# Small chunk inside the first wide chunk's steps, seven products in more second layers, and a scale applied at PSUM

## The chip, the cores and the metric

The kernel runs on one core of one Trainium2 chip. The metric is the device time of one execution in microseconds (us); lower is better. The engines are TensorE (PE; its weight loads are PEld), VectorE (DVE), ScalarE (ACT), GpSimd (POOL) and SyncE (SP), which issues the DMAs.

## What is computed

Three stages follow each other on 4 x 576 = 2304 tokens of 512 numbers: windowed attention (8 heads of 64), an MLP that mixes tokens and then a channel MLP 512 -> 1536 -> 512, and a second channel MLP 512 -> 2048 -> 512 on normalized input scaled by g.

```python
def _moe_ref(x, w_tok1, w_tok2, w_ch1, w_ch2):
    xt = x.transpose(0, 2, 1)
    h = np.maximum(xt @ w_tok1, 0.0) @ w_tok2
    u = x + h.transpose(0, 2, 1)
    h2 = np.maximum(u @ w_ch1, 0.0) @ w_ch2
    return (u + h2).astype(np.float32)

def _moe2_ref(x, g_ln, w_ch1, w_ch2):
    mu = np.mean(x, axis=-1, keepdims=True)
    var = np.mean((x - mu) ** 2, axis=-1, keepdims=True)
    xn = (x - mu) / np.sqrt(var + 1e-06) * g_ln
    ch = np.maximum(xn @ w_ch1, 0.0) @ w_ch2
    return (x + ch).astype(np.float32)
```

The weights arrive as float64 and are converted on the chip. Every matmul operand is split into a high and a low part (float32r), and a product is three matmuls: high x high, high x low, low x high.

## The kernel before

**Tiles, chunks and steps.** The 2304 tokens are 18 tiles of 128. They stay in SBUF as `u` (one buffer for all 18). After attention and the token mixing, which end near 200 us, the two channel MLPs run in steps. A step takes two blocks of 128 hidden features for one chunk of tiles. The chunks are tiles 0 to 7 (wide), 16 and 17 (small), 8 to 15 (wide), in this order, for the first MLP (6 steps each) and then the second (8 steps each): 42 steps.

**First layer of a step.** For a wide chunk, `seven_products` (L1122) computes 256 features x 1024 tokens in seven products of half-size blocks, in place of eight: 7 x 6 = 42 matmuls of 512 columns. Its inputs are 14 operand pairs (seven for each half of the contraction), made by `prep_wide` (L902) from transposes of `u` (`turned`, L873; for the second MLP ScalarE normalizes into `st` first, L883), and weight sums made by `w1_of` (L975). For the small chunk, `two_blocks` (L1223) does 24 matmuls of 256 columns.

**Second layer of a step.** `second` (L1236) does six matmuls of 512 columns for each tile (48 for a wide chunk, 12 for the small one) and adds the result to `u` on VectorE (L1256). In the last chunk of the second MLP, for all steps but the last, `second_fast` (L1261) computes it in seven products as well: for two groups of tiles, 84 matmuls of 256 columns (L1288) and twelve additions (L1307). It needs sums of hidden blocks (`parts_of`, L1172), and sums of second-layer weights, which `keep_sums` (L1058) makes on GpSimd in the first wide chunk and stores to DRAM; `sums_of` (L1100) loads them. Some of its products begin from a copy in a second PSUM bank (`fork`, L1293), which is opened by one extra matmul after transposes have used that bank (L1300). The second layer of a step runs among the first-layer products of the next step; the numbers in `ns` say how many units of it follow each pair of products.

**Weights.** `load_f64` (L411) loads a block in two halves and converts it with one ScalarE and four VectorE operations (L449 to L464). `stage_w` (L538) converts blocks ahead and keeps them in DRAM at `STAGE_RATES` a step; `load_w` (L526) loads six blocks ahead, from DRAM where a block is kept. First-layer blocks of the second MLP are multiplied by g after conversion (`convert_w`, L506, L516). `w_split` makes high and low parts: ScalarE makes the high (L385), GpSimd (L403, two instructions of half width) or VectorE (L401) the low part.

**Order of work.** Each operation is handed to a planner with its cost and the engines that may do it. It computes due times backwards from TensorE's work (`ranks`), then simulates all engines in time and fixes the engine of each operation and the order on every queue. Each queue runs in that order: an instruction that waits holds those behind it. SP's DMA issues are one such queue; `shift_wt1` (L583) issues six copies of first token-mixing weights, shifted by 64 rows, from GpSimd.

Of the kernel before, what the change touches and what calls it, by code (L numbers as in the profile page):

```python
# [51 lines left out]
FAST2 = ((1, 2),)  # L52
# [56 lines left out]
class Part(Buf):  # L109


    def __init__(self, whole, get):
        self.plan, self.pool, self.spec = whole.plan, whole.pool, whole.spec
        self.ops, self.track, self.after, self.behind, self.first = [], {}, [], None, set()
        self.whole, self.get = whole, get
# [6 lines left out]
class Plan:  # L122
# [32 lines left out]
    def op(self, cost, emit, reads=(), writes=(), behind=()):  # L155
        k = len(self.ops)
        deps, behind = set(behind), set()
        for group, write in ((reads, False), (writes, True)):
            for x in group:
# [11 lines left out]
                assert not getattr(b, "closed", False), f"{b.spec[2]} is used after its place was given away"  # L171
                assert write or any(w for key2, (w, _) in b.track.items() if key is None or key2 in (None, key)), \
                    f"{b.spec[2]} is read before it is written"
                b.ops.append(k)
                for key2, (ws, rs) in b.track.items():
# [162 lines left out]
def block_kernel(tc, qT, kT, v, wt1, wt2, wa1, wa2, wb1, wb2, g, bias, out):  # L338
# [13 lines left out]
    for name in ("const", "big", "wa", "raw", "cvt", "small", "hid"):  # L352
        open_pool(name)
# [12 lines left out]
    g_sb = buf("const", [P, DM // P, 1], F32, "g_sb")  # L366
# [6 lines left out]
    u_all = buf("big", [P, NTILE, DM], F32, "u")  # L373
    u = [Part(u_all, lambda t, i=i: t[:, i]) for i in range(NTILE)]
# [131 lines left out]
    def convert_w(x, dst=None, get=None):  # L506

        m, f = x
        if m != "b1":
            return load_f64(src[m], f, DM, dst, get)  # L510
        y, gy = load_f64(src[m], f, DM)
        if dst is None:
            dst, get = y, gy

        def scale(e):
            ENGINE[e].tensor_tensor(get().rearrange("p (k f) -> p k f", k=4), gy().rearrange("p (k f) -> p k f", k=4),  # L516
                                    g_sb.t.to_broadcast([P, 4, P]), ALU.mult)

        pl.op({"DVE": dve(DM), "POOL": pool_tt(DM)}, scale, [y, g_sb], [dst])
        return dst, get  # L520
# [187 lines left out]
    def normalize(i):  # L708
# [13 lines left out]
        minus(u[i], lambda: u[i].t.rearrange("p (h d) -> p h d", h=H), pv,  # L722
# [3 lines left out]
    def x_tile(i):  # L726
# [3 lines left out]
        split(xh, lambda: xh.t, xl, lambda: xl.t, u[i], lambda: u[i].t, DM, ("ACT",),  # L730
# [32 lines left out]
    def tok2(i):  # L763
# [18 lines left out]
        op({"DVE": dve(DM)}, lambda: nc.vector.tensor_tensor(u[i].t, o.t, u[i].t, ALU.add), [o], [u[i]])  # L782
# [6 lines left out]
    def attention():  # L789
# [37 lines left out]
        for i in range(-1, NTILE + 1):  # L827
# [15 lines left out]
            for c in range(2):  # L843
# [10 lines left out]
                if n == 1:  # L854
                    load_bias(2, 4)
                    load(g_sb, lambda: g_sb.t.rearrange("p k o -> p (k o)"), P * DM // P * 4, g)
# [16 lines left out]
    def turned(layer, places):  # L873
# [4 lines left out]
        get = [lambda i=i, k=k: u[i].t[:, k * P:(k + 1) * P] for i, k in places]  # L878
# [17 lines left out]
    def split_x(x, b, psum):  # L896

        hi, lo = x
        copy(hi, lambda: hi.t, b, lambda: b.t, CW, ("ACT",), psum)
        minus(lo, lambda: lo.t, b, lambda: b.t, hi, lambda: hi.t.bitcast(F32), CW, ("DVE",) if psum else ("DVE", "POOL"))  # L900

    def prep_wide(layer, tiles):  # L902
# [12 lines left out]

        def temp():
            return buf("mlp", [P, CW], F32, "st", ST_BUFS)

        def pieces(kk):
            b11, b12 = quadrant(0, 0, kk), quadrant(0, 1, kk)  # L920
            c12, t1 = temp(), temp()
            copy(c12, lambda: c12.t, b12, lambda: b12.t, CW, ("ACT",), True)
            split_x(part(0, kk), b11, True)
            minus(t1, lambda: t1.t, c12, lambda: c12.t, b11, lambda: b11.t, CW, ("DVE",))
            split_x(part(3, kk), t1, False)
# [3 lines left out]
            minus(t2, lambda: t2.t, b22, lambda: b22.t, t1, lambda: t1.t, CW, ("DVE",))  # L929
# [564 lines left out]
```

## Time and profile before

| | us |
|---|---|
| three runs | 833.47, 833.73, 835.28 |
| median | 833.73 |
| profiled execution, its own time | 835.53 |
| its span, first to last instruction | 833.8 |
| TensorE busy | 821.5 |
| VectorE busy | 659.1 |
| GpSimd busy | 466.9 |
| ScalarE busy | 428.5 |

The durations come from the profiled execution. In rows of instructions the second number is the duration; instructions of one engine overlap a little, so the distance between starts is shorter. An arrow `<-` names inputs, or, in rows of waits, what ended the wait. "x84" counts instructions.

### The profile page before, as it was taken

What the parts mean: (1) busy time and instruction counts of PE and PEld (TensorE: products, weight loads), DVE (VectorE), ACT (ScalarE), POOL (GpSimd) and SP (SyncE); (2) the same over time, 40 slices, a digit from 0 to 9 for tenths busy, and PEclk for the clock granted to TensorE, in tenths of its full rate; (3) what the DMA queues carried; (4) which work ended last, traced back from release to release, by engine and by line L of the source; (5) the groups of instructions that cost most, each with busy time, mean ns of one, the idle gap of its engine ahead of it and who ended that gap; (6) DMA issues with size and microseconds to landing.
All of it is one profiled execution on the core that took longest, in us unless ns stands there. A gap on an engine that the chain in (4) does not pass through costs nothing.

```text
span 833.8 us, 14352 instructions
## 1 busy us (share of the span) xinstructions
PE 821.5 (99%) x4732; PEld 693.4 (83%) x4732; DVE 659.1 (79%) x1379; ACT 428.5 (51%) x1015; POOL 466.9 (56%) x723
## 2 busy tenths in 40 slices
PE   8999999999999999999999999999999999999998
PEld 6777788888888898888888888888889889999996
DVE  5888777978787989987889868989666767777785
ACT  5888677643344535334368333447456634444430
POOL 2785466756354567544248666857533656666640
PEclk9999999999999999999999999999999999999999
DMA  9679645454678899987861544888977663443302
GB/s 328 191 184 306 232 140 191 143 186 144 216 226 297 293 317 322 339 293 240 280 238 54 188 154 139 290 309 300 354 263 237 226 226 130 137 141 116 102 26 101
DMA packets 80474, 179.21 MB, mean 215 GB/s; under 512 B 9104, under 2 KB 10768, under 8 KB 80400
## 3 DMA queue, kind: packets, MB, share of 16 engines
q1 hardware_dynamic: 79920, 176.98, 62.9%
q0 software_dynamic: 480, 1.31, 0.7%
q8 instruction: 37, 0.61, 0.3%
q14 instruction: 37, 0.30, 0.1%
HBM read 138.15 MB, written 38.80 MB: 212 GB/s over the span
## 4 chain that ended last, share of the span: by engine, by line
PE 92%; DVE 4%; ACT 3%; DMA 1%; issue 1%; POOL 0%; DVEq 0%; ACTq 0%; POOLq 0%
PE tok L1253 10%; PE tok L1251 10%; PE b L1138 10%; PE tok L1252 10%; PE b L1139 10%; PE b L1140 10%; PE tok L1288 5%; PE p L1288 4%; PE ps_s L636 3%; PE ps_v L648 3%; PE p L891 2%; PE b L482 2%; PE b L481 2%; PE b L480 2%; PE ps_t L693 1%; ACT pr L686 1%
## 5 line engine op out<-in xcount | busy, mean ns | idle before, releaser
L1256 DVE TENSOR_TENSOR u<-tok,u 128x512 f32<-128x512 f32 x196 | 134.4, 687 | 52.5 <-PE tok L1253 51.1
L1251 PE MATMUL tok<-w2h,hh 128*128 128x512 f32 x392 | 154.0, 393 | 0.0
L1253 PE MATMUL tok<-w2h,hl 128*128 128x512 f32 x392 | 152.9, 390 | 0.2 <-DVE hl L971 0.2
L1252 PE MATMUL tok<-w2l,hh 128*128 128x512 f32 x392 | 152.8, 390 | 0.0
L1138 PE MATMUL b<-xh,w1h 128*128 128x512 f32 x384 | 150.4, 392 | 0.3 <-DVE b L401 0.3
L1139 PE MATMUL b<-xl,w1h 128*128 128x512 f32 x384 | 149.8, 390 | 0.0
L1140 PE MATMUL b<-xh,w1l 128*128 128x512 f32 x384 | 149.6, 389 | 0.0
L403 POOL TENSOR_TENSOR w1l<-w,w1h 128x256 fp32r<-128x256 f32 (+1 forms) x112 | 78.9, 726 | 111.4 <-ACT w1h L385 103.4
L969 ACT ACTIVATE hh<-b 128x512 fp32r<-128x512 f32 (+1 forms) x112 | 58.7, 542 | 136.8 <-PE b L1140 95.5
L1253 PEld LDWEIGHTS tok<-w2h,hl 128*128 128x128 f32 x392 | 73.6, 188 | 16.4 <-DVE hl L971 0.8
L1251 PEld LDWEIGHTS tok<-w2h,hh 128*128 128x128 f32 x392 | 73.7, 188 | 15.1 <-DVE u L1256 0.8
L971 DVE SCALAR_TENSOR_TENSOR hl<-b,hh 128x512 fp32r<-128x512 f32 (+1 forms) x112 | 67.2, 617 | 23.9 <-ACT hh L969 23.2
L1252 PEld LDWEIGHTS tok<-w2l,hh 128*128 128x128 f32 x392 | 73.7, 188 | 14.3
L1140 PEld LDWEIGHTS b<-xh,w1l 128*128 128x128 f32 x384 | 72.1, 188 | 15.4
L1138 PEld LDWEIGHTS b<-xh,w1h 128*128 128x128 f32 x384 | 72.2, 188 | 14.6 <-DVE b L401 0.7
L1139 PEld LDWEIGHTS b<-xl,w1h 128*128 128x128 f32 x384 | 72.2, 188 | 13.5
L449 ACT ACTIVATE e<-rh 128x512 bf16<-128x512 bf16 (+2 forms) x62 | 39.7, 641 | 69.4 <-DMA rh<-wb 22.2
L403 POOL TENSOR_TENSOR w1l<-st,w1h 128x256 fp32r<-128x256 f32 x58 | 44.9, 795 | 47.9 <-ACT w1h L385 42.0
L686 ACT ACTIVATE pr<-t,mn 128x128 f32<-128x128 f32 x144 | 55.8, 391 | 14.1 <-DVE mn L677 14.0
L704 POOL TENSOR_SCALAR_AFFINE_SELECT pf<-pf 128x512 f32<-128x512 f32 x64 | 42.1, 659 | 34.6 <-ACT pf L385 28.3
L401 DVE TENSOR_TENSOR b<-b,p 128x512 f32<-128x512 f32 x56 | 38.9, 695 | 20.1 <-PE b L1140 19.5
L403 POOL TENSOR_TENSOR xl<-st,xh 128x256 fp32r<-128x256 f32 x48 | 39.0, 834 | 21.0 <-ACT xh L385 16.6
(193 smaller groups left out, 1919.9 us busy)
## 6 DMA issues: line engine op xcount, KB each, us to landing
w<-d SPq DMA_DIRECT2D x86, 256.0 KB, 4.2
rw<-wb SPq DMA_DIRECT2D x32, 512.0 KB, 5.4
rh<-wb SPq DMA_DIRECT2D x32, 512.0 KB, 5.2
rw<-wa SPq DMA_DIRECT2D x24, 512.0 KB, 4.3
rh<-wa SPq DMA_DIRECT2D x24, 512.0 KB, 4.3
d<-y SPq DMA_DIRECT2D x30, 256.0 KB, 5.3
keys<-kT SPq DMA_DIRECT2D x18, 256.0 KB, 4.6
q<-qT SPq DMA_DIRECT2D x18, 256.0 KB, 4.9
```

The source lines that it names most:

```text
L403: ENGINE[e].tensor_tensor(get()[:, c], ga()[:, c], gb()[:, c], alu)
L686: op({"ACT": 580}, lambda m=m: nc.scalar.activation(out=pr.t[:, m], in_=t.t[:, m], func=AF.Exp, bias=mn.t[:, m:m + 1], scale=-1.0, accum_o ...
L969: op({"ACT": act(n, True)}, lambda: nc.scalar.activation(out=hh.t[:, c], in_=go(), func=AF.Relu), [o], [(hh, key)])
L971: mark[0] = op({"DVE": dve(n)}, lambda: nc.vector.scalar_tensor_tensor(out=hl.t[:, c], in0=go(), scalar=0.0, in1=hh.t[:, c].bitcast(F32), ...
L1138: nc.tensor.matmul(g.t, wh.t[:, w], xh.t, start=start and k == 0, stop=False, skip_group_check=True)
L1139: nc.tensor.matmul(g.t, wh.t[:, w], xl.t, start=False, stop=False, skip_group_check=True)
L1140: nc.tensor.matmul(g.t, wl.t[:, w], xh.t, start=False, stop=stop and k == 1, skip_group_check=True)
L1251: nc.tensor.matmul(o.t, hh.t[:, c:c + P], wh.t, start=j == 0, stop=False)
L1252: nc.tensor.matmul(o.t, hh.t[:, c:c + P], wl.t, start=False, stop=False)
L1253: nc.tensor.matmul(o.t, hl.t[:, c:c + P], wh.t, start=False, stop=j == 1)
L1256: op({"DVE": dve(DM)}, lambda o=o, i=i: nc.vector.tensor_tensor(u[i].t, o.t, u[i].t, ALU.add), [o], [u[i]])
L1288: nc.tensor.matmul(o.t[:, p], x()[:, c], y(), start=start and p == 0 and k == 0, stop=stop and p == 1 and k == 2, skip_group_check=True)
```

## The change

The wide chunks become tiles 2 to 9 and 10 to 17; tiles 0 and 1 are the small chunk. There are 28 steps: the first wide chunk and the second, for each MLP. In each step of the first wide chunk the first layer of the small chunk (`small_block`) is done with the same split weight blocks, after the third pair of products and after the last product, and its two tiles are two further units of the second layer. For this the fourth first-layer block is split whole. The small chunk's inputs have places of their own.

In the first wide chunk of the second MLP the second layer of steps 1 to 6 is done in seven products too. The weight sums are then used where `keep_sums` makes them, in a pool `rows`. Tiles 10 to 17 rest in that pool: after the first step of that chunk, their statistics made, they are stored to DRAM (`put_away`), their places hold sums, and in its last step they are loaded back (`bring_back`). `u` is nine buffers of two tiles.

The scale g is no longer multiplied into the weights; it is applied where the transposed input is copied from PSUM, as a column operand of ScalarE copies and VectorE remainders. The inputs of a wide chunk are all prepared in the last step of the chunk before. Staging in the first chunk goes from 0 to 3 blocks a step. The shifted weight copies are issued by SP instead of GpSimd.

```diff
-W1_BUFS, W2_BUFS, ST_BUFS, H_BUFS = 4, 4, 6, 6
+W1_BUFS, W2_BUFS, ST_BUFS, H_BUFS = 4, 4, 6, 7
+SCRATCH = 2048
+RESTING = range(10, 18)
+SMALL, WIDE = range(2), {0: range(2, 10), 2: range(10, 18)}
-STAGE_RATES = {(0, 2): 2, (1, 0): 2}
+STAGE_RATES = {(0, 0): 3, (0, 2): 2, (1, 0): 2}
-FAST2 = ((1, 2),)
+FAST2 = {(1, 2): range(7), (1, 0): range(1, 7)}
...
-        for c, tiles in enumerate((range(8), (16, 17), range(8, 16))):
+        for c, tiles in WIDE.items():
...
-                nc.gpsimd.dma_start(out=b.t[D:], in_=a.t[:D])
-                nc.gpsimd.dma_start(out=b.t[:D, 1:], in_=a.t[D:, :4])
-                nc.gpsimd.dma_start(out=b.t[:D, 0], in_=a.t[D:, 4])
-
-            op({"POOL": 3900}, emit, [(a, k) for k in range(5)], [b])
+                x, y = a.t.bitcast(F32), b.t.bitcast(F32)
+                nc.sync.dma_start(out=y[D:], in_=x[:D])
+                nc.sync.dma_start(out=y[:D, 1:], in_=x[D:, :4])
+                nc.sync.dma_start(out=y[:D, 0], in_=x[D:, 4])
+
+            op({"DMA": 1820}, emit, [(a, k) for k in range(5)], [b])
...
+    def copy_x(dst, get, b, gb, f):
+
+        if f is None:
+            return copy(dst, get, b, gb, CW, ("ACT",), True)
+        op({"ACT": act(CW, True, 1)}, lambda: nc.scalar.activation(
+            out=get(), in_=gb(), func=AF.Copy, scale=g_sb.t[:, f]), [b, g_sb], [dst])
+
+    def less(dst, get, b, gb, a, ga, f):
+
+        if f is None:
+            return minus(dst, get, b, gb, a, ga, CW, ("DVE",))
+        op({"DVE": dve(CW)}, lambda: nc.vector.scalar_tensor_tensor(
+            out=get(), in0=gb(), scalar=g_sb.t[:, f], in1=ga(), op0=ALU.mult, op1=ALU.subtract), [b, g_sb, a], [dst])
...
-            w3 = w_split("w1", W1_BUFS, f2, right(f2), HW)
+            w3 = w_split("w1", W1_BUFS, f2) if whole else w_split("w1", W1_BUFS, f2, right(f2), HW)
...
+    def in_rows():
+
+        x, y = (buf("rows", [P, 2, DM], F32R, "r", len(RESTING) // 2) for _ in range(2))
+        return [[(z, k), lambda z=z, k=k: z.t[:, k]] for z in (y, x) for k in range(2)]
...
+    def put_away(tiles):
+        for i in tiles:
+            d = resting[i] = buf("dram", [P, DM], F32, f"r{i}")
+            op({"DMA": 728}, lambda x=u[i], d=d: nc.sync.dma_start(out=d.t, in_=x.t), [u[i]], [d])
+
+    def bring_back(tiles):
+        for i in tiles:
+            if i % 2 == 0:
+                pair_of_rows(i // 2)
+            op({"DMA": 728}, lambda x=u[i], d=resting[i]: nc.sync.dma_start(out=x.t, in_=d.t), [resting[i]], [u[i]])
...
         product(6, bd, False, end)
         out(0, 1, bd)
         yield
+        if small:
+            hid["small"] = hidden()
+            small_block(0, ws[0][0], small, hid["small"])
+            yield
         product(5, bb, False, end)
         out(1, 0, bb)
+        if small:
+            yield
+            small_block(1, ws[5][0], small, hid["small"])
         yield
...
+        ns = (6, 8, 0, 0) if before and fast2(before[0]) else (2, 3, 3, 0)
+        if c == 0:
+            ns = (6, 8, 0, 2) if before and fast2(before[0]) else (2, 3, 3, 2) if fast2(s) else (2, 3, 3, 0, 1, 1)
...
+        if before and n == 0 and steps[s - 1][0] == 0:
+            done = steps[s - 1][2]
+            for tiles in (done, SMALL) if steps[s - 1][1] == 0 else (done,):
+                todo.extend((tile_stats, i) for i in tiles)
+                todo.append((chunk_stats, tiles))
+            if layer == 1:
+                while todo:
+                    do_next()
+                put_away(RESTING)
+        if (layer, c) == (1, 0) and n == NF2 // 2 - 1:
+            bring_back(RESTING)
...
+        if end:
             while todo:
                 do_next()
-            if c == 0:
-                xs = prep_small(layer, steps[s + 1][2])
-            else:
-                xs, pieces = prep_wide(1, steps[s + 1][2])
-                for _ in pieces:
-                    pass
+            xs, pieces = prep_wide(*steps[s + 1][::2])
+            for _ in pieces:
+                pass
+            if steps[s + 1][1] == 0:
+                small = prep_small(1, SMALL)
```

## Rows read from the trace of the kernel before

**Rows 1.** The page, part 1: busy time, share of the span, instructions:
```profile
PE 821.5 (99%) x4732; PEld 693.4 (83%) x4732; DVE 659.1 (79%) x1379; ACT 428.5 (51%) x1015; POOL 466.9 (56%) x723
```

**Rows 2.** Waits of TensorE, 200 to 834 us: total, times, longest:
```profile
PE tok L1288 <- DVE u L1256: 0.4, 1, 0.4
PE b L1138 <- DVE b L401: 0.3, 1, 0.3
PE tok L1253 <- DVE hl L971: 0.2, 1, 0.2
```

**Rows 3.** Timeline of TensorE: start us, us; 156 matmuls apart:
```profile
229.70 0.39 PE L1251 MATMUL tok<-w2h,hh 128*128 128x512 f32 x1
...
265.06 1.03 PE L891 MATMUL p<-ident,u 128*128 128x128 f32 x8
```

**Rows 4.** The chain that ended last, one same place in two successive steps:
```profile
708.33 1.43 PE tok L1288 x12
...
727.91 1.43 PE tok L1288 x12
```

**Rows 5.** Timeline of TensorE, small chunk: one same place in two steps:
```profile
625.05 0.28 PE L480 MATMUL b<-fewh,w1h 128*128 128x256 f32 x1
...
630.69 0.28 PE L480 MATMUL b<-fewh,w1h 128*128 128x256 f32 x1
```

**Rows 6.** Stretches: us; busy PE, PEld, DVE, ACT, POOL (instructions); clock, DMA share, GB/s:
```profile
70.00:80.00 10.00, 8.62 (x80) 6.72 (x76) 8.19 (x40) 8.68 (x31) 5.73 (x14) 1.00 0.92 312
...
322.00:342.00 20.00, 19.68 (x86) 15.77 (x85) 18.92 (x38) 7.74 (x14) 15.72 (x25) 1.00 0.97 351
...
443.00:463.40 20.40, 20.40 (x98) 16.59 (x97) 19.57 (x35) 15.02 (x33) 16.06 (x26) 1.00 0.28 94
...
524.60:545.00 20.40, 20.24 (x90) 16.44 (x89) 19.15 (x32) 7.92 (x15) 17.59 (x28) 1.00 0.83 288
...
708.33:727.91 19.58, 19.58 (x128) 17.81 (x128) 14.70 (x23) 9.16 (x17) 12.97 (x20) 1.00 0.40 135
```

**Rows 7.** Groups of VectorE by line and shape: busy, mean ns, idle before:
```profile
L1256 DVE TENSOR_TENSOR u<-tok,u 128x512 f32<-128x512 f32 x196 | 134.4, 687 | 52.5 <-PE tok L1253 51.1
...
L456 DVE TENSOR_SCALAR m<-rw 128x512 uint32<-128x512 uint32 x56 | 32.8, 586 | 0.9 <-DMA rw<-wb 0.7
...
L464 DVE SCALAR_TENSOR_TENSOR y<-m,s 128x512 f32<-128x512 uint32 x36 | 29.5, 819 | 1.2 <-POOL w L516 0.9
...
L454 DVE SCALAR_TENSOR_TENSOR s<-e,s 128x256 int32<-128x256 int32 x56 | 29.3, 524 | 0.2
...
L452 DVE TENSOR_SCALAR s<-e 128x256 int32<-128x256 int32 x56 | 21.6, 385 | 2.7 <-ACT e L449 2.5
```

**Rows 8.** Groups of GpSimd by line and shape:
```profile
L403 POOL TENSOR_TENSOR w2l<-w,w2h 128x256 fp32r<-128x256 f32 x42 | 33.8, 826 | 15.7 <-ACT w2h L385 15.5
...
L403 POOL TENSOR_TENSOR fewh<-fewh,fewl 128x256 fp32r<-128x256 f32 x28 | 22.7, 836 | 0.0
...
L403 POOL TENSOR_TENSOR fewh<-w,fewh 128x128 f32<-128x128 f32 x28 | 14.1, 526 | 0.0
```

**Rows 9.** Groups of ScalarE by line and shape:
```profile
L883 ACT ACTIVATE st<-u,nmr,rstd 128x128 f32<-128x128 f32 x72 | 29.5, 488 | 0.0
...
L385 ACT ACTIVATE xh<-p 128x512 fp32r<-128x512 f32 x24 | 14.2, 597 | 10.7 <-PE p L891 5.8 <-DVE st L401 3.4 <-PE b L1140 1.5
```

**Rows 10.** DMA issues (KB, us to landing); SP queue's waits after 210 us:
```profile
d<-y SPq DMA_DIRECT2D x30, 256.0 KB, 5.3
...
SPq L1051 <- PE tok L1288: 35.0, 13, 11.7
```

**Rows 11.** Timeline of GpSimd, first issue of the shifted copies:
```profile
53.30 0.76 POOL L587 DMA_DIRECT2D wt1h<-wt1h  x1
```

**Rows 12.** Timeline of GpSimd in the first wide chunk, second MLP:
```profile
512.88 1.89 POOL L403 TENSOR_TENSOR w2l<-w,w2h 128x256 fp32r<-128x256 f32 x2
...
518.16 1.43 POOL L403 TENSOR_TENSOR w2l<-w,w2h 128x256 fp32r<-128x256 f32 x2
```

More of the change, by code (lines that the diff above doesn't have):

```diff
@@ L113, in __init__ @@
         self.plan, self.pool, self.spec = whole.plan, whole.pool, whole.spec
-        self.ops, self.track, self.after, self.behind, self.first = [], {}, [], None, set()
+        self.ops, self.track, self.after, self.behind, self.first = [], {}, whole.after, whole.behind, set()
         self.whole, self.get = whole, get
@@ L170, in op @@
                     behind.add(b.behind.ops[0])
-                assert not getattr(b, "closed", False), f"{b.spec[2]} is used after its place was given away"
+                assert not getattr(getattr(b, "whole", b), "closed", False), f"{b.spec[2]} is used after its place was given away"
                 assert write or any(w for key2, (w, _) in b.track.items() if key is None or key2 in (None, key)), \
@@ L350, in open_pool @@
         pl.pools[name] = tc.alloc_tile_pool(name=name, **{"bufs": 1, **kw})
-    for name in ("const", "big", "wa", "raw", "cvt", "small", "hid"):
+    for name in ("const", "big", "rows", "wa", "raw", "cvt", "small", "hid"):
         open_pool(name)
@@ L977, in w1_of @@
         f1, f2 = take_w(), take_w()
-        if len(steps[s][2]) == 2:
-            out = [w_split("w1", W1_BUFS, x) for x in (f1, f2)]
-            keep_taken(2)
-            return out
+        whole = steps[s][1] == 0
         if ahead == "few":
@@ L1053, in w2_of @@
             out.append(x)
-        if c == 0 and (layer, 2) in FAST2 and n < (NF1, NF2)[layer] // 2 - 1:
-            keep_sums(layer, n, wtiles[used[0] - 2:used[0]], last)
-        return sums_of(layer, n, out) if fast2(s) else out
-    def keep_sums(layer, n, w, last):
+        if c == 0:
+            if n not in FAST2.get((layer, 2), ()):
+                return out
+            places = in_rows() if fast2(s) else in_few()
+            keep_sums(layer, n, wtiles[used[0] - 2:used[0]], last, *places)
+            return with_sums(out, *quarters(*places)) if fast2(s) else out
@@ L1096, in keep_sums @@
+        for k, (l, gl), (h, gh) in ((0, lo0, hi0), (1, lo1, hi1)):
+            if k:
+                sub(0, half(x0, 1), half(x1, 1))
+                sub(1, half(x1, 0), part(1))
+            else:
+                sub(0, half(x0, 1), half(x0, 0))
+                sub(1, half(x1, 1), part(0))
+            split(h, gh, l, gl, f, lambda: f.t, DM, ("ACT",), ("POOL",))
+            for p, z, gz in (("h", h, gh), ("l", l, gl)):
                 op({"DMA": 728}, lambda k=k, p=p, gz=gz: nc.sync.dma_start(
-                    out=d[p].t[:, k * DM:(k + 1) * DM], in_=gz().bitcast(F32)), z, [(d[p], k)], last)
+                    out=d[p].t[:, k * DM:(k + 1) * DM], in_=gz().bitcast(F32)), [z], [(d[p], k)], last)
@@ L1454, in block_kernel @@
         pl.emit()
-    for n in ("mlq", "mlr", "mlp", "even", "psc", "pst", "psm", "hid", "small", "cvt", "raw", "wa", "big", "const", "dram"):
+    for n in ("mlq", "mlr", "mlp", "even", "psc", "pst", "psm", "hid", "small", "cvt", "raw", "wa", "rows", "big", "const", "dram"):
         pl.pools[n].release()
```

213 lines of the change are left out of this document (107 added, 106 removed).

## The prediction

> **What bounds the kernel now.** I read the page first: TensorE is busy 99% of the span, the next engine, VectorE, 79% [rows 1]. So time can be won only by fewer or shorter matmuls, and lost only by making TensorE wait. The waits say where it waits today: after 200 us only three times, 0.9 us together [rows 2]. Then the pace. From 229.70 to 265.06 stand 156 back-to-back matmuls of 512 columns, 226.7 ns each [rows 3]. A step of a wide chunk has 42 of them in its first layer and 48 in its second: 90 x 0.2267 = 20.40 us. Where the second layer is done in seven products (tiles 8 to 15, second MLP), 84 matmuls of 256 columns stand for the 48, and the chain repeats every 19.58 us [rows 4]. A step of the small chunk repeats after 5.64 us [rows 5]. These periods contain what is lost at each change of width, so I use them and not durations of single matmuls, which overlap.
>
> **The change part by part.**
> *Seven products in six more steps.* Six steps go from 20.40 to 19.58 us on TensorE: 6 x 0.82 = -4.9. The second-layer banks must be opened again in the first wide chunk: two more matmuls of 512 columns (line 1300) at the pace of rows 3, +0.45. The Trainium skill (TensorE: Matmul & The Clock Gate, Back-to-back issue gap) puts an isolated gap at N/2.4 + 2.5 ns; as an estimate from that page a step would save 48 x 215.8 - 84 x 109.2 ns = 1.19 us, the six 7.1, and the sum below would end at 828.6. The trace shows slower paces for both widths, 226.7 ns for 512 columns, and decides.
>
> *Small chunk inside the wide steps.* Its matmuls stay, 5.64 us a step, 14 times: 0. What goes is its own weight work: in each of its steps two loads of first-layer blocks, four of second-layer parts, two splits; 84 loads of 256 KB in all. The hand-over from small to wide chunk at 322 to 342 us, with VectorE busy 18.9 of 20, left TensorE idle 0.32 us [rows 6]; that place disappears: -0.3 (bounds 0 and -0.9, the three waits of rows 2).
>
> *Load of VectorE and GpSimd in the new steps.* This is the main unknown. A step with seven products now holds 14.70 us of VectorE and 12.97 of GpSimd [rows 6]. In the first wide chunk of the second MLP there come on top, for VectorE: two float64 conversions (385 + 524 + 586 + 819 ns = 2.31 each) 4.6, two more additions of 687 ns 1.4, two ReLU remainders of half width, at most as long, 1.4 [rows 7]: 22.1. For GpSimd: the weight sums, eight pieces of 0.526 and four of 0.836, 7.6; the low parts of two second-layer blocks, four of 0.826, 3.3; half a block more of the first layer, under one such piece, 0.8 [rows 8]: 24.7. Together 46.8 of 2 x 25.2 us (19.58 + 5.64), 93% at most; the planner can move the low parts between the two. The nearest row is 524.60 to 545.00: 19.15 + 17.59 of 2 x 20.40, 90%, with 0.16 us of TensorE idle [rows 6]. Five steps have the whole load (steps 2 to 6; step 1 ends with plain second-layer work of step 0): 5 x 0.16 = +0.8. Bounds: 0 (443 to 463 us, 87%, no idle [rows 6]) and +7.3, the first rival.
>
> *Scale g at PSUM.* Sixteen multiplications go from VectorE and GpSimd; in their place ScalarE copies and VectorE remainders that exist already take a column as scale. The trace has no copy of that form; the nearest row is the normalizing activation with two columns, 488 ns for 128 columns [rows 9], against 597 for 512 columns without: a column can cost at most what the narrow one costs, 0.5 us on 20 copies, 10 us of ScalarE over two hand-overs, and at least nothing. I take 0: ScalarE was busy 15 of 20.4 us in such a place [rows 6]; without that cover it goes into the third hand-over below.
>
> *Staging three weights a step in the first chunk.* By the order of uses in the code 19 conversions fall there instead of 14: 0.8 x 2.31 = 1.9 us more of VectorE in steps longer by 5.64. 0.
>
> *Prepared inputs at three hand-overs.* The 14 operand pairs of a wide chunk were prepared during the small chunk; now all between the last product of one chunk and the first of the next. The trace has one such place, into the second MLP at 443 to 463 us: VectorE 19.57 of 20.40, ScalarE 15.02, TensorE not idle [rows 6]. From chunk to chunk in the first MLP, and into the second, now with the small inputs too, I take 0.2 each, between that 0 and the 0.32 at 322. The third is harder: tiles 10 to 17 come back from DRAM, and the places of the last two pairs, and the transposes' banks, are free only when the seven products of step 6 are done, some 15 us into step 7. From there TensorE has 23 us of other work (three products 4.1, small blocks and tiles 5.6, ten tiles of 1.36). ScalarE needs three quarters of 32 x 0.488 + 16 x 0.597 = 25.2 [rows 9], 19, and about 5 for its own step. About even: +0.6. The three together +1.0; bounds 0 and 3 x 1.4, the largest loss shown anywhere (70 to 80 us, 8.62 busy of 10 [rows 6]).
>
> *Resting tiles.* Eight stores and eight loads of 256 KB on SP's queue (5.3 us to landing for such a store [rows 10]) come, against 84 loads gone. The stores wait for the statistics of the tiles, now made in one step instead of over several; behind them on SP stand the weight loads of the next step. SP waits up to 11.7 us today without TensorE noticing [rows 10]. 0; without that cover it is the second rival.
>
> *Copies of the shifted weights.* Six DMA issues, the first 0.76 us [rows 11], leave GpSimd for SP; there they wait for the last split of the weights, and q, k, v and raw loads stand behind them. Soon after, at 70 to 80 us, TensorE loses 1.4 of 10 us [rows 6]. Bounds -1.4 and +1.4; nothing singles out a sign: 0.
>
> **Sum:** -4.9 + 0.45 - 0.3 + 0.8 + 1.0 = -2.95. The profiled execution has a span of 833.8 and took 835.53 us, 1.8 above the median of the runs, 833.73; the change is small beside that, so I take it from the median: **830.8 us**.
>
> **The rivals.**
> *Slower: VectorE and GpSimd fill up in the first wide chunk of the second MLP.* For it: a pair of GpSimd pieces took 1.43 us at 518.16 and 1.89 at 512.88 [rows 12]. If all ran at 1.89, where the mean is 2 x 0.826, the 24.7 become 28.2, 3.0 over the 25.2; with half of that taken by VectorE the step grows by 1.5. It decides as soon as the two together need more than 50.4. Five steps: +7.3 in place of +0.8: **837.3**. Against it: 90% was carried with 0.16 lost. Chance 0.19. The Trainium skill (SBUF — State Buffer, Who interferes with whom) states that a VectorE instruction with two SBUF inputs contends with a GpSimd instruction that reads SBUF, and that the later one blocks fully; the trace shows a third more for a pair, not a whole instruction's wait each time.
> *No difference: the tiles come back late.* If SP issues the last loads behind another wait, 5 us of landing lie ahead of ScalarE's 24, against 23 of cover; less what the first two pairs allow, some 3 us of TensorE idle between steps 7 and 8 instead of 0.6: **833.2**. Against it: the first two pairs' places are free a step earlier. Chance 0.20.
> *The full gain:* hand-overs and load cost nothing and all three waits of rows 2 go: 833.7 - 4.9 + 0.45 - 0.9 = **828.4**; with luck in attention 827. For it: the hand-over at 443 cost nothing. Chance 0.12.
>
> **The numbers.** Forecast 0.49. A measurement of this kernel tells about 0.2%, 1.7 us, from no change, so faster begins under 832.1: forecast and full gain together, 0.61, less a little of the forecast's upper edge, give 0.60; within 0.2% 0.21; slower 0.19. The range goes from 827.0 to 837.0: full gain, forecast and no difference lie in it, the slower rival with its lower half. The likeliest case's own range is 829 to 832.
>
> **What would show it.** The line of the seven products (1288) has 588 matmuls now and has 588 + 6 x 84 = 1092 after; the chain repeats after about 25.2 us in steps 2 to 6 of that chunk. If it is longer there, and TensorE's waits name lines of VectorE or GpSimd, the first rival holds. A TensorE gap before the first products of the last chunk, behind transposes or ScalarE, is the second. The prediction is wrong altogether if TensorE waits in the first MLP, or if attention ends over 1.5 us earlier or later.

## The result and the profile after

The change makes the kernel slower: median 842.82 us (841.55 to 845.12) against 833.68 for the kernel before in the same comparison, ratio 1.0109, 95% interval 1.0082 to 1.0135. The forecast was 830.8 and the range ended at 837.0. The profiled execution has a span of 843.4 (before: 833.8). It is the slowest of the four, at a mean granted clock of 0.996; the one that took 841.55 had 1.00.

Part 1 of the page after, which answers to [rows 1]:

```profile
PE 821.8 (97%) x4950; PEld 700.0 (83%) x4950; DVE 686.3 (81%) x1422; ACT 442.9 (53%) x1031; POOL 450.7 (53%) x692
```

TensorE is as busy as before in us, but the busy time holds stalls in flight, so this row alone hides what happened. The waits of TensorE over the whole span tell more (where [rows 2] had three waits of 0.9 us after 200 us):

```profile
PE b L1197 <- DVE hl L1012: 4.0, 5, 1.7
PE tok L496 <- POOL xl L418: 2.7, 2, 2.4
PE ps_s L641 <- DMA q<-qT: 2.2, 1, 2.2
...
PE p L1354 <- DVE hl L416: 1.1, 1, 1.1
PE p L899 <- ACT st L891: 1.0, 1, 1.0
```

L1197 is a first-layer product, L496 the token mixing in attention, L1354 the seven products of the second layer, L899 the transposes. The wait for q lies at the very start: the product behind it begins at 8.62 us, against 7.70 before, with the same instructions ahead of it. So time went in three different stages. The stretches show it, first of the kernel before, then of the one after (columns as in [rows 6]):

```profile
20.00:30.00 10.00, 9.71 (x100) 7.86 (x100) 9.69 (x38) 8.91 (x36) 7.49 (x15) 1.00 0.68 220
...
190.00:340.00 150.00, 149.68 (x742) 126.41 (x741) 129.62 (x230) 65.14 (x122) 86.88 (x124) 1.00 0.79 268
...
440.00:640.00 200.00, 199.84 (x951) 167.08 (x950) 159.10 (x266) 98.25 (x199) 125.78 (x192) 1.00 0.67 229
655.00:700.00 45.00, 44.62 (x246) 38.77 (x245) 30.43 (x51) 20.65 (x40) 22.77 (x33) 1.00 0.53 176
```

```profile
20.00:30.00 10.00, 7.43 (x62) 5.40 (x61) 7.93 (x28) 6.74 (x30) 4.80 (x9) 0.92 0.68 216
...
190.00:340.00 150.00, 147.39 (x714) 123.58 (x713) 118.43 (x204) 56.94 (x105) 66.12 (x104) 1.00 0.72 249
...
440.00:640.00 200.00, 198.24 (x1182) 175.64 (x1180) 179.20 (x296) 111.44 (x218) 146.11 (x216) 1.00 0.58 198
655.00:700.00 45.00, 42.51 (x210) 34.60 (x209) 33.18 (x51) 33.27 (x69) 20.50 (x29) 0.96 0.49 166
```

TensorE is idle 2.3 us more at 20 to 30 us, 2.3 more in the first chunk of the first MLP, 1.6 more at 440 to 640, 2.1 more at 655 to 700; and at the first and the last place the granted clock was lower too.

For a balance by stage I use **lost time**: the length of a stretch less what its matmuls need at the pace of [rows 3] (226.7 ns for 512 columns; 117.9 for 256, the pace of the seven products). It comes from the starts of all matmuls of one profiled execution, so it shares that execution's luck; the start of the kernel alone varies by 1 us from run to run. In attention narrow matmuls start in pairs, some 7 ns apart, so up to 190 us only differences between kernels mean something.

| lost us | to 190 | 190-440 | 440-640 | 640-700 | 700-end | all | matmul work |
|---|---|---|---|---|---|---|---|
| before | 16.1 | 1.7 | 1.6 | 1.1 | 1.0 | 21.5 | 808.2 |
| after | 19.9 | 4.8 | 4.5 | 6.7 | 1.1 | 36.9 | 802.7 |

The work fell by 5.5 us, as intended; 15.4 us more are lost. Three places account for nearly all of it, and each can be read in the trace.

**Attention, 20 to 33 us.** The chain of the kernel after:

```profile
20.67 4.23 DMA g_sb<-g
24.89 0.08 issue
24.97 0.23 POOL g_sb L864
25.20 0.08 issue
25.28 0.24 POOL rc L725
25.51 0.08 issue
25.59 1.42 POOL xl L418 x2
27.01 0.04 issue
27.05 0.50 PE tok L496
```

The full change has an operation that the prediction passed over: behind g's load GpSimd multiplies g by -1 (L864, 128x4, 0.23 us). It waits 4.23 us for the load; `rc` and the low part `xl`, whose high part ScalarE had made by 21.8 us, stand behind it on GpSimd's queue, and TensorE waits for `xl`.

**Step changes in the first wide chunks.** Timeline around 294 us, rows of TensorE, ScalarE and VectorE:

```profile
287.22 0.28 PE L497 MATMUL b<-xsh,w1l 128*128 128x256 f32 x1
...
291.40 0.28 PE L497 MATMUL b<-xsh,w1l 128*128 128x256 f32 x1
...
292.68 0.39 PE L1199 MATMUL b<-xh,w1l 128*128 128x512 f32 x1
...
293.11 1.64 ACT L1010 ACTIVATE hh<-b 128x512 fp32r<-128x512 f32 x4 [4.99 <-PE b L1199]
...
293.74 1.95 DVE L1012 SCALAR_TENSOR_TENSOR hl<-b,hh 128x512 fp32r<-128x512 f32 x4 [2.42 <-ACT hh L1010]
...
294.81 0.50 PE L1197 MATMUL b<-xh,w1h 128*128 128x512 f32 x1 [1.74 <-DVE hl L1012]
```

The last matmul of the first small block started at 287.22, that of the second at 291.40, yet ScalarE sat idle for 4.99 us and then read four results out in a row. Product 6 of the first layer (last matmul at 292.68) had been put last by the planner. The hidden tiles are a ring of seven that is handed out in order (`buf` sets `b.behind = ring[-1]`), and the small block's tile follows that of product 6: it can't be read out before it. The next step's first product needs the small block's PSUM bank and waits for all of it.

**The third hand-over.** Transposes of the last chunk (L899) and the loads that bring the tiles back (L1125): count, ns (least, median, most), first and last start; and ScalarE preparing the first inputs:

```profile
L899 PE MATMUL p<-ident,st x32: 270/272/331, 652.7 to 682.4; 128*128 128x128 f32 x32
...
L1125 SPq DMA_DIRECT2D r<-r x8: 319/402/427, 626.3 to 652.0; - x8
...
635.28 1.26 ACT L891 ACTIVATE st<-r,nmr,rstd 128x128 f32<-128x128 f32 x3
```

All 32 transposes come from 652.7 us on, with nine tiles and two small blocks of TensorE work left before the last chunk's first product (674.8 us), beside a serial chain of ScalarE and VectorE. For the first four the tiles were not what was late: ScalarE had normalized them by 636.5 us. What came in between is the seven products of step 6, which use the transposes' banks up to 650.5 us. TensorE runs dry at 664 us, and then the timeline shows matmuls at half pace:

```profile
663.57 0.40 PE L1319 MATMUL tok<-w2h,hl 128*128 128x512 f32 x1
664.98 1.48 PE L899 MATMUL p<-ident,st 128*128 128x128 f32 x4 [1.02 <-ACT st L891]
666.65 0.79 PE L1317 MATMUL tok<-w2h,hh 128*128 128x512 f32 x1 [0.18 <-DVE u L1322]
667.23 0.63 PE L1318 MATMUL tok<-w2l,hh 128*128 128x512 f32 x1
...
670.40 0.40 PE L1317 MATMUL tok<-w2h,hh 128*128 128x512 f32 x1
670.63 0.40 PE L1318 MATMUL tok<-w2l,hh 128*128 128x512 f32 x1
```

From 667.23 to 669.8 the starts are 0.43 us apart, at 670.4 again 0.23: the lower of the two levels of the clock, 1.2 GHz, after 2.7 us with only four transposes. The granted clock of that stretch:

```profile
667.20:670.20 3.00, 3.00 (x9) 2.36 (x8) 2.00 (x3) 3.00 (x8) 2.30 (x4) 0.52 0.58 221
```

### The profile page after: what moved, and what is told of

It is laid out like the page before. It is cut to its first block, busy times and chain, and to the rows that moved or that the text cites. A ratio compares the mean times of both kernels' runs of the same rounds, so it can differ in the third digit from the quotient of the medians.

```text
span 843.4 us, 14729 instructions
## 1 busy us (share of the span) xinstructions
PE 821.8 (97%) x4950; PEld 700.0 (83%) x4950; DVE 686.3 (81%) x1422; ACT 442.9 (53%) x1031; POOL 450.7 (53%) x692
## 4 chain that ended last, share of the span: by engine, by line
PE 88%; DVE 4%; DMA 4%; ACT 2%; issue 1%; POOL 1%; SPq 0%; DVEq 0%; ACTq 0%
PE b L1197 11%; PE b L1198 10%; PE b L1199 10%; PE tok L1354 8%; PE tok L1317 8%; PE tok L1318 8%; PE tok L1319 8%; PE p L1354 7%; PE ps_v L653 3%; PE ps_s L641 3%; PE ps_t L698 1%; PE p L899 1%; DMA q<-qT 1%; PE b L497 1%; PE b L496 1%
## 5 line engine op out<-in xcount | busy, mean ns | idle before, releaser
L1197 PE MATMUL b<-xh,w1h 128*128 128x512 f32 x384 | 151.4, 394 | 4.2 <-DVE hl L1012 4.0
L1317 PE MATMUL tok<-w2h,hh 128*128 128x512 f32 x296 | 118.1, 399 | 0.2 <-DVE u L1322 0.2
L1318 PE MATMUL tok<-w2l,hh 128*128 128x512 f32 x296 | 116.1, 392 | 0.0
L1319 PE MATMUL tok<-w2h,hl 128*128 128x512 f32 x296 | 116.0, 392 | 0.0
L1197 PEld LDWEIGHTS b<-xh,w1h 128*128 128x128 f32 x384 | 72.2, 188 | 18.6 <-DVE hl L1012 5.6
L1322 DVE TENSOR_TENSOR u<-tok,u 128x512 f32<-128x512 f32 x92 | 63.1, 688 | 22.4 <-PE tok L1319 20.9
L1319 PEld LDWEIGHTS tok<-w2h,hl 128*128 128x128 f32 x296 | 56.0, 189 | 12.1
L1317 PEld LDWEIGHTS tok<-w2h,hh 128*128 128x128 f32 x296 | 56.0, 189 | 11.4 <-DVE u L1322 0.4
L1318 PEld LDWEIGHTS tok<-w2l,hh 128*128 128x128 f32 x296 | 56.1, 190 | 10.6
L1012 DVE SCALAR_TENSOR_TENSOR hl<-b,hh 128x512 fp32r<-128x512 f32 (+1 forms) x88 | 50.3, 597 | 17.7 <-ACT hh L1010 17.5
L418 POOL TENSOR_TENSOR w1l<-w,w1h 128x256 fp32r<-128x256 f32 (+1 forms) x62 | 44.9, 744 | 25.9 <-ACT w1h L400 24.8
L418 POOL TENSOR_TENSOR w2l<-w,w2h 128x256 fp32r<-128x256 f32 x48 | 37.5, 803 | 35.8 <-ACT w2h L400 33.6
```

Of the source, the lines that this page charges most:

```text
L418: ENGINE[e].tensor_tensor(get()[:, c], ga()[:, c], gb()[:, c], alu)
L1012: mark[0] = op({"DVE": dve(n)}, lambda: nc.vector.scalar_tensor_tensor(out=hl.t[:, c], in0=go(), scalar=0.0, in1=hh.t[:, c].bitcast(F32), ...
L1197: nc.tensor.matmul(g.t, wh.t[:, w], xh.t, start=start and k == 0, stop=False, skip_group_check=True)
L1317: nc.tensor.matmul(o.t, hh.t[:, c:c + P], wh.t, start=j == 0, stop=False)
L1318: nc.tensor.matmul(o.t, hh.t[:, c:c + P], wl.t, start=False, stop=False)
L1319: nc.tensor.matmul(o.t, hl.t[:, c:c + P], wh.t, start=False, stop=j == 1)
```

## The experiments

The theory after the trace: these three places. The rival: VectorE and ScalarE are simply too full where the small chunk stands (VectorE 179.20 of 200 us at 440 to 640, against 159.10), and waits only move. Where an operation or a due time is changed, the planner orders all queues anew, attention too; so results are read by stage. The kernel after was not timed again in these comparisons, and the median of the kernel before ranged from 833.51 to 834.81 in them; so a difference to the kernel after is good to about 1 us.

**The small operation.** Alone in the kernel before (every other instruction keeps its place on every queue), and moved to 50 us in the kernel after (the order of the other engines stays):

```diff
 b1_neg_only (kernel before; g_neg stands for an unused scratch place)
+op({"POOL": 200}, lambda: nc.gpsimd.tensor_scalar(g_neg, g_sb.t, -1.0, None, ALU.mult), [g_sb], ...)
 e1_neg_late (kernel after)
-op({"POOL": 200}, lambda: nc.gpsimd.tensor_scalar(g_sb.t[:, 4:], g_sb.t[:, :4], -1.0, ...), [], [g_sb])
+if n == 20: op({"POOL": 200}, lambda: nc.gpsimd.tensor_scalar(g_sb.t[:, 4:], ...), [u[4]], [g_sb])
```

> Kernel before, with one thing of the change alone: GpSimd multiplies g by -1 (128x4) right behind the load of g; the result is not used, and the order of all other instructions on all engines stays. Theory (the small operation waits on GpSimd's queue for g's load, about 4 us, and what stands behind it there makes TensorE wait): TensorE waits 2 to 3 us for a low part xl on GpSimd between 24 and 28 us, and the time rises from 833.7 to 836.0 to 836.8. Rival (the loss in attention comes from the other things changed there, the shifted copies on SP or the new order): no wait there, 833.3 to 834.3.

> Changed kernel, with the multiplication of g by -1 moved to about 50 us, when g has long landed; the order on all other engines stays. Theory: the wait of 2.4 us for xl at 25 us goes, the lost time up to 190 us falls from 19.9 to about 17.2 us, and the time from 842.8 to 840.1 (839.6 to 840.8). Rival (another part of the change sets attention's end, the shifted copies on SP for one): the gain at 25 us is given back by 70 us, 842.3 to 843.3.

b1_neg_only: 837.44 us, ratio 1.0039 (1.0025 to 1.0053): +2.6 on the median of before in that comparison, 834.81. Its waits at 19 to 30 us have a row that the kernel before has not, and the clock stays at 1.00:

```profile
PE tok L481 <- POOL xl L403: 2.2, 1, 2.2
...
20.00:30.00 10.00, 7.62 (x72) 5.97 (x70) 7.72 (x29) 7.71 (x30) 6.15 (x12) 1.00 0.66 227
```

e1_neg_late: 839.92 us, 1.0061 (1.0048 to 1.0075). The wait is gone and so is the fall of the clock, 1.00 in place of 0.92. First the kernel after, then e1:

```profile
25.00:30.00 5.00, 2.95 (x11) 2.02 (x13) 3.24 (x6) 1.74 (x8) 4.77 (x9) 0.84 0.40 125
30.00:40.00 10.00, 10.00 (x94) 8.15 (x94) 7.60 (x27) 6.96 (x25) 7.14 (x13) 0.91 0.49 143
...
20.00:30.00 10.00, 9.79 (x108) 8.20 (x108) 9.76 (x39) 8.45 (x33) 8.56 (x16) 1.00 0.83 281
```

Lost up to 190 us: 14.8 (after: 19.9). TensorE's order is the same in both, so each matmul can be compared with itself. In the kernel after it starts 0.6 us later than in e1 just before the wait, 3.1 right behind it and 5.0 at 33 us; from there the distance stays, between 5.0 and 5.3 up to the end. So 2.5 us are the wait, 1.9 the matmuls behind it at a granted clock of 0.84 and 0.91, and nothing later gives it back. In b1, where the clock did not fall, the same comparison with the kernel before gives 2.4 us across the wait. Both sides agree: 0.23 us of GpSimd cost about 3 us of the whole (2.6 and 2.9 by the medians; 3.3 and 4.0 by the ratios to the kernel before).

**The order of the read-outs.** e3 takes the other bank for the first small block, e5 gives product 6 an earlier due time:

```diff
 e3_one_bank
-        ps = bank(2 * j)
+        ps = bank(2)
 e5_p6_first
+        was, pl.shift = pl.shift, -30 if small else pl.shift
         product(6, bd, False, end)
+        pl.shift = was
```

> Changed kernel, with both small blocks of a step in PSUM bank 2, so that the first product of the next step, in bank 0, does not wait for VectorE to read the first small block out. Theory: the waits of that product for the small block's remainder (4.0 us in 5 waits in the whole run, 1.9 lost at the last step change of the first MLP's first chunk alone) go, and the stages from 190 to 340 and from 440 to 660 us lose 2.5 to 4 us less: 839 to 840.5 if attention keeps its 19.9 us. Rival (VectorE and ScalarE are late there with everything, and the wait only moves to the next reader): the same losses under other names, 842 to 844.

> Changed kernel, where product 6 of the first layer comes earlier in TensorE's order in the steps that hold the small chunk (only its due time in the planner is changed). Theory (the hidden tiles are handed out in order, so ScalarE can't read out a small block before product 6, and where the planner put product 6 last, four read-outs stand in a row at the end of the step, with the first product of the next step behind them): the waits for hl at line 1012 (4.0 us) fall under 0.8, the lost time from 190 to 340 us from 4.4 to under 1.5, and from 440 to 520 us from 1.7 to under 1: 838.5 to 840 with attention as in the changed kernel. Rival (VectorE and ScalarE are too full in these steps): the loss from 190 to 340 us stays over 3 us, 842 to 844.

e3_one_bank: 841.04 us, 1.0073 (1.0060 to 1.0086). Here the theory, as put, fell: 190 to 440 us lose 4.7 (after: 4.8), and the wait has a new reader, the small block itself, for 3.0 us in four waits; the gain came from a new order in attention (16.8 lost) and at the third hand-over (4.5 lost from 640 to 700 us, after: 6.7). The bank is where the wait is felt, not where it is made. e5_p6_first: 835.93 us, 1.0022 (1.0011 to 1.0033), 6.9 below the kernel after. From 190 to 640 us its waits for the small block's remainder are down to one:

```profile
PE b L1197 <- DVE hl L1012: 0.2, 1, 0.2
```

```profile
190.00:340.00 150.00, 149.76 (x732) 126.32 (x731) 117.80 (x205) 58.23 (x108) 70.02 (x108) 1.00 0.73 250
440.00:640.00 200.00, 199.60 (x1198) 177.53 (x1197) 177.13 (x297) 109.73 (x210) 154.02 (x228) 1.00 0.61 211
```

The engines hold the same load as in the kernel after (VectorE 177.13 of 200), and TensorE is idle 0.2 and 0.4 us instead of 2.6 and 1.8. 190 to 440 us lose 1.4 instead of 4.8, 440 to 640 us 2.7 instead of 4.5. The order was the cause there, not the load. (2.3 us of its gain lie in attention and 1.8 at the third hand-over, by the new order.)

**The third hand-over.** e2 makes all second layers of that chunk plain, e4 only the last but one step's, with the loads a step earlier, e6 is e2 with late loads:

```diff
 e2_plain_10
-FAST2 = {(1, 2): range(7), (1, 0): range(1, 7)}
+FAST2 = {(1, 2): range(7)}
 e4_five
+FAST2 = {(1, 2): range(7), (1, 0): range(1, 6)}
-        if (layer, c) == (1, 0) and n == NF2 // 2 - 1:
+        if (layer, c) == (1, 0) and n == NF2 // 2 - 2:
 e6_tiles_late (on e2_plain_10)
-                    ..., [resting[i]], [u[i]])
+                    ..., [resting[i]] + ([x] if i > 13 else []), [u[i]])   # x = hid[1, 0][0]
```

> Changed kernel, with the second layer of the first wide chunk of the second MLP in plain matmuls again (the small chunk stays in its steps, tiles still go to DRAM and back). TensorE's work grows by 4.5 us. Theory (the seven products hold the row places and the two banks of the transposes until late in the last step, and this is what makes the inputs of the last chunk late): the lost time from 655 to 700 us, 5.5 in the changed kernel, falls under 1.5, that of steps 6 and 7 (1.7) under 0.5, and the time stays within 841 to 843.5. Rival (the hand-over is too full without the small chunk's steps, whatever the second layer is): 4 us or more stay lost there, and the time is 846 or more.

> Changed kernel, with seven products in steps 1 to 5 of the first wide chunk of the second MLP instead of 1 to 6, and the resting tiles brought back from the last step but one. TensorE's work grows by 0.8 us. Theory (row places and the transposes' banks, held by the seven products of step 6, make the third hand-over late): the lost time from 655 to 700 us falls from about 6 to under 1.5 us, and the time to 838 to 839.5 with attention as in the changed kernel. Rival (the two added vector engines' loads in the last steps are what is late): 4 us or more stay lost there, 842 to 844.

> The kernel of e2_plain_10 (plain second layer in the first wide chunk of the second MLP), with the last four resting tiles fetched only after product 5 of the last step is read out, about when the changed kernel fetches them; the transposes' banks are as free as in e2_plain_10. If the late tiles alone make the third hand-over late: 3 to 6 us are lost from 655 to 700 us, as in the changed kernel (6.2), and the time is 845 to 848. If it is the banks (or ScalarE behind them): under 1.5 us are lost there, 841 to 842.5, as in e2_plain_10.

e2_plain_10: 841.70 us, 1.0087 (1.0074 to 1.0100); 0.4 us lost from 640 to 700 (after: 6.7), but 5.2 from 440 to 640: with another order, product 6 stands last in most of these steps, and the waits for hl come back (2.9 us, six). e4_five: 838.22 us, 1.0054 (1.0038 to 1.0070); 0.7 lost from 640 to 700. That points at the seven products of step 6, but e4 moves the loads as well; m4 and m5 below differ in step 6 alone. e6_tiles_late was to tell the row places from the transposes' banks and did not: 866.34 us, 1.0398 (1.0376 to 1.0419), because the planner now put product 6 last in nearly all steps (waits for hl 18.3 us in twelve), and 28 of the 32 transposes start from 682.1 us on, 28 us after the late loads were issued (653.0 to 654.4). In the kernel after, the first four transposes waited for no tile (above); for the others, whose last four tiles were fetched at 650.7 to 652.0 us, it stays open which of the two holds them back.

**All three together, and the planner's costs.** m1 joins e1, e4 and e5. a3 and b3 change no operation, only two costs in the planner, in the kernels after and before; m3 adds to a3 the repairs of m1 (with -15 for -30, and the loads where the kernel after has them):

```diff
 a3_costs, b3_costs, m3_costs
-    LAT = {"PE": 400, "DVE": 260, "ACT": 290, "POOL": 180, "DMA": 4000, "CTL": 0}
+    LAT = {"PE": 400, "DVE": 140, "ACT": 170, "POOL": 180, "DMA": 4000, "CTL": 0}
-    return 2.6 + n / 2.4
+    return 13 + n / 2.4
```

> Changed kernel with three edits together: the multiplication by -1 at 50 us (e1_neg_late), product 6 earlier (e5_p6_first), and seven products in steps 1 to 5 with the tiles fetched one step earlier (e4_five). If these three places hold what the change loses: 829 to 832, faster than the kernel before by 2 to 4 us, with the seven-product steps' gain of 5 x 0.8 us left over. Rival (the losses only move on to other waits): 834 or more.

> Changed kernel; only the planner's costs are set to what the traces show: a matmul of 512 columns 226 ns instead of 216, and 120 ns less for a result to pass from VectorE or ScalarE on. No operation is added or removed. Theory (the losses of the changed kernel are orders that the planner chose for times that are not the chip's; product 6 last in a step is one): the waits for hl at line 1012 fall from 4.0 to under 1.5 us; the third hand-over keeps 4 to 6 us; 837 to 840. Rival (the orders are right and the engines too full): 842 to 844.

> Kernel before with the same two edits of the planner's costs, as the measure for a3_costs. If the kernel before had already the order that suits the chip: 833 to 836, no gain. If it too loses by the wrong costs: up to 2 us faster, 831.5 to 833.

> a3_costs with the three repairs: the multiplication by -1 at 50 us, product 6 earlier in the steps with the small chunk, seven products in steps 1 to 5 only. If the three places and the orders hold what the change loses: up to 190 us 15 us lost, 190 to 640 us under 4, 640 to 700 us under 2.5, 828 to 831. Rival (losses move on to other waits, as in m1_three): 834 or more.

All four missed. m1_three: 839.43 us, 1.0055 (1.0038 to 1.0072): 14.5 lost up to 190 and 0.7 from 640 to 700, as expected, but 7.5 from 440 to 640, with five waits for hl, 5.5 us, in other steps than before the repair (below). a3_costs: 847.81 us, 1.0166 (1.0153 to 1.0179): the waits for hl fell to 1.8, and others came, 21.9 lost up to 190 us. b3_costs: 837.53 us, 1.0048 (1.0030 to 1.0066): the same costs make the kernel before slower. m3_costs: 836.73 us, 1.0027 (1.0014 to 1.0040). Costs nearer to the chip's don't make better orders by themselves. After these the rival, engines too full, still stood.

What m1's new waits have in common with the old ones shows before 551.5 us, where TensorE waits 1.57 us for hl:

```profile
539.91 0.28 PE L497 MATMUL b<-xsh,w1l 128*128 128x256 f32 x1
...
544.33 0.63 ACT L400 ACTIVATE w1h<-st 128x512 fp32r<-128x512 f32 x1 [4.91 <-PE tok L1321]
...
548.27 0.63 ACT L400 ACTIVATE hh<-st 128x512 fp32r<-128x512 f32 x1
548.79 0.38 ACT L1010 ACTIVATE hh<-b 128x256 fp32r<-128x256 f32 x1
```

Product 6 stands early here. The first small block's last matmul starts at 539.91, and its read-out comes at 548.79, right behind a hidden sum of the seven products (`hh<-st`), whose tile stands just before it in the same ring. So the ring holds the read-out back in either case; what stands ahead of it differs.

**Settling it.** m4 has e1's and e4's edits (without the earlier loads) and ties the first small block early as well as product 6; m5 is m4 with six steps, m6 is m4 with none:

```diff
 m4_order
+FAST2 = {(1, 2): range(7), (1, 0): range(1, 6)}
+        was, pl.shift = pl.shift, -10 if small else pl.shift
         product(6, bd, False, end)
+        pl.shift = was
...
+            was, pl.shift = pl.shift, -10
             small_block(0, ws[0][0], small, hid["small"])
+            pl.shift = was
 m5_order6: FAST2 as in the kernel after
 m6_plain: FAST2 = {(1, 2): range(7)}
```

> Changed kernel with the multiplication by -1 at 50 us, seven products in steps 1 to 5 only, and both product 6 and the first small block (with its read-out) given earlier due times in the planner. If the order of the read-outs, the hand-over and the small operation hold what the change loses: lost up to 190 us 14 to 15 us, 190 to 440 us under 2.5, 440 to 640 us under 3.5, 640 to 700 us under 1.5; 828.5 to 831.5, faster than the kernel before. Rival (VectorE and ScalarE are too full in the steps that hold the small chunk, so the waits only move, as in m1_three and m3_costs): 440 to 640 us lose 4 us or more, 834 or more.

> m4_order with seven products in steps 1 to 6, as in the changed kernel. If the sixth step costs the third hand-over: 640 to 700 us lose 4 to 6 us instead of under 1.5, less the 0.8 of one step: 832 to 835. Rival (with the orders mended the hand-over has time for six steps): under 2 us lost there, 828 to 830.

> m4_order with a plain second layer in the first wide chunk of the second MLP. TensorE's work is 4.5 us more than in m4_order. If the five steps' load costs nothing once the orders fit: 3.5 to 5 us slower than m4_order. Rival (the load of VectorE and GpSimd takes most of the gain back, wherever the read-outs stand): within 1.5 us of m4_order.

m4_order: **830.07 us**, ratio 0.9952 (0.9940 to 0.9965), faster than both kernels. Its page and stretches:

```profile
PE 817.0 (99%) x4914; PEld 696.7 (84%) x4914; DVE 668.4 (81%) x1397; ACT 440.8 (53%) x1024; POOL 466.3 (56%) x720
```

```profile
190.00:340.00 150.00, 150.00 (x730) 126.45 (x729) 117.49 (x202) 58.53 (x110) 70.12 (x108) 1.00 0.70 237
...
440.00:640.00 200.00, 199.32 (x1163) 175.59 (x1162) 175.65 (x298) 110.17 (x211) 149.97 (x224) 1.00 0.66 230
655.00:700.00 45.00, 45.00 (x253) 39.31 (x252) 33.44 (x52) 21.45 (x41) 24.58 (x39) 1.00 0.52 179
```

VectorE 175.65 and GpSimd 149.97 of 200 us, together as full as in the kernel after (179.20 and 146.11), and TensorE idle 0.7. With e5, which has all six steps, the rival falls as the cause of these waits. Some price of the seven products is left in the stage: it loses 2.3 us without them (m6), 3.5 with five steps, 4.2 with six (m5). The transposes are spread over the end of the chunk instead of standing behind it:

```profile
L899 PE MATMUL p<-ident,st x32: 270/272/273, 622.1 to 656.4; 128*128 128x128 f32 x32
```

m5_order6: 835.51 us, 1.0014 (1.0003 to 1.0024). The sixth step alone costs 5.4 us, and the hand-over, where 5.9 us more are lost than in m4_order, looks as in the kernel after (transposes from 643.7 us on; 6.5 lost from 640 to 700):

```profile
655.00:700.00 45.00, 42.60 (x214) 35.17 (x215) 33.84 (x51) 29.84 (x60) 21.86 (x31) 0.96 0.35 121
```

m6_plain: 833.63 us, 1.0001 (0.9992 to 1.0010). Against it the five steps of m4_order are worth 3.6 us; and with the small operation moved and the read-outs in order, the rest of the change (small chunk inside, g at PSUM, tiles to DRAM and back) comes out even with the kernel before.

**The shifted copies**, alone in the kernel before (the three copies of each pair as in the diff of the change):

```diff
 b2_shift_sp
-                nc.gpsimd.dma_start(out=b.t[D:], in_=a.t[:D])
+                nc.sync.dma_start(out=y[D:], in_=x[:D])
...
```

> Kernel before, with one thing of the change alone: the six copies that shift the token weights are issued by SP instead of GpSimd (the planner's order shifts a little with it). The prediction's term was 0, between -1.4 and +1.4. Theory now (attention's loss is the small GpSimd operation): no more than 0.7 us either way, 833.1 to 834.5. Rival (SP's queue, with q, k and v behind the copies, is part of attention's loss): over 1 us more lost between 50 and 80 us, 835 or more.

832.94 us, 0.9981 (0.9972 to 0.9991): a little faster, 14.9 lost up to 190 us (before: 16.1). SP's queue bears them.

The stages of the runs that carry the verdicts, in lost us as above:

| | to 190 | 190-440 | 440-640 | 640-700 | 700-end | all | matmul work |
|---|---|---|---|---|---|---|---|
| e1_neg_late | 14.8 | 4.8 | 4.7 | 6.4 | 1.0 | 31.6 | 802.7 |
| e5_p6_first | 17.6 | 1.4 | 2.7 | 4.9 | 1.0 | 27.5 | 802.7 |
| e4_five | 20.1 | 1.6 | 5.6 | 0.7 | 1.0 | 29.1 | 803.7 |
| m1_three | 14.5 | 3.1 | 7.5 | 0.7 | 1.0 | 26.8 | 803.7 |
| m4_order | 13.2 | 2.2 | 3.5 | 0.6 | 1.0 | 20.4 | 803.7 |
| m5_order6 | 14.4 | 1.7 | 4.2 | 6.5 | 1.0 | 27.8 | 802.7 |
| m6_plain | 13.6 | 2.2 | 2.3 | 0.7 | 1.0 | 19.7 | 808.2 |

## Why the prediction was wrong

**Seven products in six more steps, -4.9 + 0.45: right in size.** m6_plain to m4_order is -3.6 for five steps, 0.71 each; without the 0.45 for the opening matmuls 0.80, near the 0.82 from [rows 3, 4]. The Trainium skill (TensorE: Matmul & The Clock Gate, Back-to-back issue gap) gave, as the prediction's estimate, 1.19 a step; the measured 0.80 doesn't bear that out.

**"Scale g at PSUM ... I take 0": the first step that failed.** The sum counted multiplications that go and column operands that come, and left out the one operation that is new on a queue, the multiplication of g by -1. It should have been asked what stands behind it there, as the prediction did for SP. It cost about 3 us, where the sum had 0 (2.6 by b1_neg_only, 2.9 by e1_neg_late). The column operands themselves were near nothing: the ScalarE copies with one took 0.69 us (median of L908) against 0.597 [rows 9], 0.09 each, inside the bounds.

**"Small chunk inside the wide steps ... Its matmuls stay: 0": the second.** The count of matmuls was right. Missing was that two more results a step pass through ScalarE, VectorE and a ring handed out in order, and that the planner chooses where product 6 stands. Where the sum had 0, 190 to 640 us lost 6.0 us more than before; moving one due time gave 5.2 of it back (e5_p6_first).

**"Prepared inputs at three hand-overs, +1.0": the third, and the largest.** The third hand-over was described rightly (places and banks free late, some 15 us into step 7, ScalarE's 24 us against 23 of cover) and then called "about even: +0.6". The sixth step's hand-over cost 5.4 net of that step's own gain (m5_order6 against m4_order). The work in the other queues did not fit under its cover evenly: TensorE ran dry at 664 us in the middle of the serial chain of transposes, copies and remainders, and the clock fell to its lower level on top of it. The second rival named the place (3 us of idle time there, 833.2), gave late loads as the reason, which the first four transposes do not bear out, and had the size too small as well.

**"Load of VectorE and GpSimd in the new steps, +0.8", and the first rival, 837.3.** The rival had the right sign and the wrong cause. The two steps between 532.5 and 583.0 us, whose read-outs were in order, took 25.3 and 25.2 us, as forecast. The first of them, in the kernel after:

```profile
532.50:557.80 25.30, 25.30 (x165) 23.03 (x164) 23.96 (x38) 14.13 (x27) 22.08 (x34) 1.00 0.87 310
```

VectorE and GpSimd were busy for 46.0 us together, near the 46.8 computed, and TensorE was not idle at all. (The rival's five steps of 1.5 us also make 7.5, not 7.3.)

**Resting tiles, 0; shifted copies, 0.** No wait of TensorE names one of the stores. The copies gained a little (b2_shift_sp) instead of costing. Staging three blocks a step was not tried alone.

The signs that the prediction named as fatal were the ones that came: TensorE waits in the first MLP (2.5 us for hl at 190 to 345 us), and attention ends 1.7 us later (first wide step at 160.9 instead of 159.2). Together: -4.3 for six steps, 6.1 for the hand-over (5.4 and the 0.7 that it hid), 2.6 for the operation and about 5 for the read-outs make +9.4; measured +9.1. The fit is better than its parts deserve, and partly luck: every new plan also shifts attention (lost up to 190 us: 13.2 to 21.9 in these runs).

## What to carry to other kernels

Price an added instruction by what stands behind it on its queue until its input lands, not by its duration: 0.23 us on GpSimd cost about 3. Where queue orders are fixed by a planner, a change that adds results to read out has a second price, the order it provokes; look in the trace for a producer that stands last in a step and for a ring that makes others wait for it, and mend the due time before judging the idea. A preparation that has "about as much" cover as it needs did not fit here: try giving up the last step's gain to free its places earlier (five steps gave 3.6 us, the sixth cost 5.4).

## What the runs showed of the hardware that was not expected

The clock made two of the losses larger than the waits. After 2.7 us with only four transposes, matmuls started 0.43 us apart instead of 0.23 for some 2.6 us (granted clock 0.52 over that stretch). Behind the 2.4 us wait in attention the granted clock was 0.84 and 0.91 up to 40 us, and the matmuls there fell back by another 1.9 us; behind the same wait of 2.2 us in b1_neg_only it stayed at 1.00, and the matmuls fell back by only 0.2 us more. So a wait of one length had two prices.

A load of 2 KB (g, four numbers in each of 128 rows) took 4.23 us from issue to landing, about as long as 256 KB in the same kernel: the medians on its page are 4.5 us for a load from the kept weights and 3.8 for a store.
